# Pooled attention and two feed-forward layers: second batch's first steps held back by two units, value tails in three buffers, y staged in the weight sums' buffer, last sums stored by sync

## The chip, the core and the metric

One core of a Trainium2 chip runs the whole program. The metric is the device time of one execution in microseconds (us); less is better. The core's engines are TensorE (PE in the profile, with its weight loads as PEld), VectorE (DVE), ScalarE (ACT), GpSimd (POOL) and SyncE (SP), which issues nearly all DMAs. Each engine works through its own instructions in the order in which the program writes them and waits for the others by semaphores.

## What is computed

```python
k_p = k.reshape(B, H, Sp, pool, D).mean(axis=3)      # B, H, S, D = 8, 8, 576, 64; pool = 8, Sp = 72
v_p = v.reshape(B, H, Sp, pool, D).mean(axis=3)
attn = softmax(scale * q @ k_p.T)
x = (attn @ v_p) as 4608 tokens x 512
h = x @ w_in                                         # 512 x 2048
y = (h * clip(h + 3, 0, 6) / 6) @ w_out              # 2048 x 512
g = y @ w_gate; val = y @ w_val                      # 512 x 1536 each
out = (silu(g) * val) @ w_out2                       # 1536 x 512
```

The weights arrive as float64 words and are turned into fp32 on the chip. All products are taken in fp32 precision, as three products of a high and a low part (`mm3`, `split`).

## The kernel before

The work stands in one hand-written order (`manual_schedule`): a line that comes later in the program is queued later on its engine.

**Attention and first layer, up half.** Tokens go in nine blocks `j` of 512 (`NB`). Block 0's attention runs alone at the start. From then on, while TensorE makes the 16 products `up(hp, wu[f], x_tile(j))` of block `j` (one for each group `f` of 128 columns of `w_in`), `attn_slot` runs the attention of block `j + 1` in between, two slots for each `f`. The attention is cut into 84 units (a head pair and some rows), and each unit into steps with one letter: P brings q into the transposed layout (`prep_q`), RK and K pool and transpose k, R0 and R1 pool v and v's tail on GpSimd, R and Q split v, S are the scores, X A N M the softmax, E F T U L V W Y the transposes and the product with v. `when` and `when_startup` give each step a due time of unit number plus lag, and `steps` is sorted by it. So the list decides what stands ahead of what on every engine, and `block_end[j]`, the place of a block's last Y, decides which steps are done before block `j`'s products begin. Unit 8 and 9 are the last 64 rows of batch 0; unit 10 is the first of batch 1.

**Loads of the attention.** A load is put off by a number of steps after the step that frees its buffer (`later`): q of segment `i + 2` 12 steps after P of segment `i`, v's tail two heads and v three heads ahead, both 4 steps after Q. The tails have two buffers (`vts_t`), v has three. All are issued by SP in that order. R1 (tail of head h) and R0 (v of head h + 1) stand one behind the other on GpSimd, ahead of F of a unit with an even number (VectorE has the odd ones); F makes the low part of the unit's tail columns, which T's second transposes on TensorE (line 563) need.

**Weights.** In block 0 `weights.convert` brings one more group of `w_in` per `f`: ScalarE rescales a fetched tile, VectorE joins the words, and SP fetches the next into the freed tile. The other weights are turned into seven sums per tile by `prep_step` in steps spread over the blocks (`prep_slot`); tiles `q7` and `s7` hold a tile and its sums, and the sums go to memory. The gated block is stored by `store_g` from four `g32` tiles, one `f` behind.

**First layer, down half (stage b).** It runs for all nine blocks after the last up products, in seven products a block (`down_b`, n = 0 to 6). Its first operands, ten loads of 1 MB (`first_loads`: four `gq` tiles, six halves of `pw` tiles), are issued in `f` = 0 to 9 of the last block, and eight more halves directly after it. `split_b` makes the high and low parts, `evac_b` adds the products up to y and stores y; in the last block y is stored from ScalarE's queue. Four weight pieces are still prepared in this stage.

**Second layer.** It runs in six groups `p` of 768 tokens. `load_y` brings y into a tile, `x_step` makes seven operands in `xc` (quarters 11, 12, 21, 22 and their differences T1 to T4) by a copy on ScalarE (line 147), a subtraction on VectorE (line 148) and a difference (line 210). `up2` (line 694) takes them in the order 11, T2, T1, 21, T4, T3, 22. Weights for it come through four `wr` ring tiles (`load_next`). All these tiles are laid out where stage b's `gq`, `pw`, `stg`, `q7` and `s7` tiles stood, so their first loads wait until those have been read. At the change from stage b to the second layer the first group's `load_y`, `load_next` and `x_step`s are placed by hand behind n = 5 and n = 6 of the last block, after `evac_b`.

Of the kernel before, what the change touches and what calls it, by code (L numbers as in the profile page):

```python
# [23 lines left out]
def kernel(  # L24
# [27 lines left out]
    nc = tc.nc  # L52
# [25 lines left out]
    prep_ctx = ExitStack()  # L78
    stg_p = prep_ctx.enter_context(tc.tile_pool(name="stg", bufs=3, side="right"))
    q7_p = prep_ctx.enter_context(tc.tile_pool(name="q7", bufs=1, side="right"))  # L80
    s7_p = prep_ctx.enter_context(tc.tile_pool(name="s7", bufs=1, side="right"))
# [133 lines left out]
    WH = WC // 2  # L215
    prep_t = {}
# [12 lines left out]
    def prep_step(u, step):  # L229
# [21 lines left out]
        elif step in (2, 3):  # L251
            if step == 2:
                prep_t["f", u] = q7_p.tile([P, 8, WH], F32, tag="q7", name="q7")
# [8 lines left out]
        elif step in (5, 6):  # L262
            if step == 5:
                prep_t["s", u] = s7_p.tile([P, 7, 2, WH], F32R, tag="s7", name="s7")
# [31 lines left out]
    vts_t = [a_p.tile([96, POOL, D], F32, name=f"vts{i}") for i in range(2)]  # L296
    vmask = a_p.tile([P, 2, D], F32, name="vmask")
# [24 lines left out]
    def load_vtail(b, p, eng):  # L322
        v1 = v[b, 2 * p + 1].rearrange("(s o) d -> s o d", o=POOL)
        vts = vts_t[p % 2]
# [111 lines left out]
    def prep_v(b, p):  # L436
# [4 lines left out]
            out=m, in0=t[:, 0:1].to_broadcast([P, 2, D]), in1=vmask, op=ALU.mult  # L441
# [202 lines left out]
    def load_y(p):  # L644

        t = l2["ys"].tile([P, 4, 2, M], F32, tag="ys", name="ystg")
# [6 lines left out]
    def x_step(p, n, lo_eng, sum_eng):  # L653
# [4 lines left out]
        what, then = [("11", "T1"), ("22", "T3"), ("T1", "T2"), ("21", "T4"), ("T2", None), ("T3", None), ("T4", None)][n]  # L658
        x = xc[p, what] = l2["x"].tile([P, 2, 2, M], F32R, tag="x" + what, name="xc")
# [164 lines left out]
    lb = {}  # L824
# [54 lines left out]
    def evac_b(j, n):  # L879
# [91 lines left out]
    events = []  # L971
    for i in range(NU):
        startup_unit = i < unit_end[0]
        lag = dict(when_startup if startup_unit else when)
# [8 lines left out]
        events += [(i + lag[st[0]][0], lag[st[0]][1], st[1], n, st) for n, st in enumerate(stages)]  # L983
# [20 lines left out]
    for i, h in ((i, head_no[u[0], p]) for i, u in enumerate(units) for p in u[1]):  # L1004
# [8 lines left out]
        if h + 2 < len(heads) and h >= KT - 1:  # L1013
            before(("Q", h), ("R1", h + 2))
# [297 lines left out]
```

## Time and profile before

| | us |
|---|---|
| median of 3 runs | 1797.77 (1796.95 to 1799.96) |
| profiled execution | 1801.43 |
| its span | 1799.6 |
| PE busy in it | 1717.7 (95%) |
| DVE, ACT, POOL busy | 1336.2, 754.4, 634.7 |
| mean granted TensorE clock | 0.979 of full speed |

Matmuls of lines 609, 873 and 694 (up half, stage b, second layer) make nearly all of PE's time. TensorE is the engine that is nearly always busy; the time that can be won lies in its waits and in stretches where its granted clock is low.

### The profile page before, as it was taken

What the parts mean: (1) busy time and instruction counts of PE and PEld (TensorE: products, weight loads), DVE (VectorE), ACT (ScalarE), POOL (GpSimd) and SP (SyncE); (2) the same over time, 40 slices, a digit from 0 to 9 for tenths busy, and PEclk for the clock granted to TensorE, in tenths of its full rate; (3) what the DMA queues carried; (4) which work ended last, traced back from release to release, by engine and by line L of the source; (5) the groups of instructions that cost most, each with busy time, mean ns of one, the idle gap of its engine ahead of it and who ended that gap; (6) DMA issues with size and microseconds to landing.
All of it is one profiled execution on the core that took longest, in us unless ns stands there. A gap on an engine that the chain in (4) does not pass through costs nothing.

```text
span 1799.6 us, 30919 instructions
## 1 busy us (share of the span) xinstructions
PE 1717.7 (95%) x11209; PEld 1618.0 (90%) x11209; DVE 1336.2 (74%) x2356; ACT 754.4 (42%) x1657; POOL 634.7 (35%) x812
## 2 busy tenths in 40 slices
PE   4789998999999899999999899999999999999999
PEld 3568877877878699999999799999999999999999
DVE  6587887888886378888887578668568668668666
ACT  6464554555554345555554224225124124224222
POOL 6246665666732000000000252352351361450550
PEclk8799999999999999999999899999999999999999
DMA  7576878787777985554454787977977977878876
GB/s 167 123 188 174 250 227 261 237 258 229 221 225 274 393 328 187 183 182 147 161 203 150 263 275 246 318 269 244 320 256 249 328 251 257 316 247 274 274 246 214
DMA packets 235833, 432.47 MB, mean 240 GB/s; under 512 B 86689, under 2 KB 168609, under 8 KB 218529
## 3 DMA queue, kind: packets, MB, share of 16 engines
q1 hardware_dynamic: 233536, 429.20, 72.3%
q8 instruction: 88, 1.44, 0.3%
q10 hardware_dynamic: 2144, 1.31, 0.2%
q14 instruction: 65, 0.52, 0.1%
HBM read 326.11 MB, written 104.33 MB: 239 GB/s over the span
## 4 chain that ended last, share of the span: by engine, by line
PE 69%; DMA 8%; DVE 4%; issue 1%; SPq 1%; ACT 1%; POOL 1%; ACTq 0%; DVEq 0%; POOLq 0%
PE b L694 44%; PE b L873 17%; PE h L609 7%; DMA pw<-sw 1%; DMA wstg<-in_moe_w_out_dram 1%; DMA g<-g 1%; DVE g L625 1%; DMA gq<-g 1%; DMA wstg<-in_moe_w_val_dram 1%; DVE s L269 1%; DMA y<-o 1%; DMA q_in<-in_q_dram 0%; PE pss L489 0%; SPq L374 0%; DMA vts<-in_v_dram 0%
## 5 line engine op out<-in xcount | busy, mean ns | idle before, releaser
L694 PE MATMUL b<-xc,wr 128*128 128x384 f32 x3024 | 528.5, 335 | 8.6 <-ACT xc L147 5.4
L694 PEld LDWEIGHTS b<-xc,wr 128*128 128x128 f32 x3024 | 526.4, 189 | 9.5 <-ACT xc L147 5.8
L609 PE MATMUL h<-x,wu 128*128 128x512 f32 x1728 | 436.7, 404 | 9.2 <-DVE g L625 8.8
L741 POOL TENSOR_TENSOR s<-s,c 128x384 f32<-128x384 f32 x144 | 142.5, 1014 | 773.6 <-ACT s L739 773.6
L703 DVE TENSOR_TENSOR c<-c,b 128x384 f32<-128x384 f32 x504 | 265.2, 552 | 178.7 <-PE b L694 153.2
L609 PEld LDWEIGHTS h<-x,wu 128*128 128x128 f32 x1728 | 323.3, 193 | 78.5 <-DVE g L625 13.2
L873 PE MATMUL b<-gb,pw 128*128 128x256 f32 x3024 | 364.2, 283 | 3.4 <-ACT gb L147 2.8
L873 PEld LDWEIGHTS b<-gb,pw 128*128 128x128 f32 x3024 | 363.6, 192 | 4.1 <-ACT gb L147 3.0
L694 PE MATMUL b<-wr,gc 128*128 128x256 f32 x2268 | 265.6, 279 | 0.0
L694 PEld LDWEIGHTS b<-wr,gc 128*128 128x128 f32 x2268 | 265.4, 188 | 0.0
L147 ACT CAST gb<-gq 128x512 fp32r<-128x512 f32 x252 | 155.6, 621 | 170.2 <-PE b L873 159.1
L148 DVE TENSOR_TENSOR gb<-gq,gb 128x512 fp32r<-128x512 f32 x252 | 168.3, 688 | 64.0 <-ACT gb L147 63.3
L748 POOL TENSOR_TENSOR gf<-s,c 128x384 f32<-128x384 f32 x144 | 168.3, 1194 | 67.4 <-DVE c L703 64.8
L147 ACT CAST gc<-gf 128x768 fp32r<-128x768 f32 x126 | 105.7, 839 | 187.2 <-POOL gf L748 101.3
L739 ACT ACTIVATE s<-c 128x384 f32<-128x384 f32 x144 | 73.6, 526 | 204.6 <-DVE c L703 203.3
L148 DVE TENSOR_TENSOR gc<-gf,gc 128x768 fp32r<-128x768 f32 x126 | 134.1, 1096 | 15.6 <-ACT gc L147 13.9
L620 ACT ACTIVATE t<-h,half 128x512 f32<-128x512 f32 x144 | 99.2, 689 | 85.3 <-PE h L609 50.8
L625 DVE SCALAR_TENSOR_TENSOR g<-t,h 128x512 f32<-128x512 f32 x144 | 97.5, 677 | 33.5 <-DMA g<-g 23.5
L711 ACT COPY c<-b 128x384 f32<-128x384 f32 x72 | 33.9, 471 | 143.9 <-PE b L694 143.9
L851 DVE TENSOR_TENSOR gq<-gq 128x1024 f32<-128x1024 f32 x72 | 87.7, 1219 | 0.0
L537 POOL TENSOR_TENSOR e<-e,sm 128x288 f32<-128x288 f32 (+4 forms) x73 | 47.4, 649 | 110.1 <-DVE sm L533 85.5
L489 PE MATMUL pss<-kbd,qT 128*128 128x144 f32 (+2 forms) x320 | 58.1, 304 | 20.2 <-DVE qT L471 16.5
(106 smaller groups left out, 1673.1 us busy)
## 6 DMA issues: line engine op xcount, KB each, us to landing
wr<-sup SPq DMA_DIRECT2D x72, 1024.0 KB
wr<-sdn SPq DMA_DIRECT2D x84, 768.0 KB
wr<-sup SPq DMA_DIRECT2D x72, 768.0 KB
g<-g SPq DMA_DIRECT2D x144, 256.0 KB
gq<-g SPq DMA_DIRECT2D x36, 1024.0 KB
sup<-s SPq DMA_DIRECT2D x12, 1792.0 KB
wstg<-in_moe_w_out_dram SPq DMA_DIRECT2D x56, 256.0 KB
sw<-s SPq DMA_DIRECT2D x8, 1792.0 KB
```

Of the source, the lines that this page charges most:

```text
L147: nc.scalar.copy(out=hi, in_=src)
L148: lo_engine.tensor_tensor(out=lo, in0=src, in1=f32(hi), op=ALU.subtract)
L609: nc.tensor.matmul(out=ps, lhsT=w(kt, wh), rhs=x(kt, xh), start=first and n == 0, stop=last and n == 3 * len(kts) - 1,)
L620: nc.scalar.activation(out=t, in_=ps, func=ACTF.Relu, bias=half, scale=1.0 / 6.0)
L625: nc.vector.scalar_tensor_tensor(out=g, in0=t, scalar=1.0, in1=ps, op0=ALU.min, op1=ALU.mult)
L694: nc.tensor.matmul(out=ps, lhsT=w(wh), rhs=x(xh), start=first and n == 0, stop=last and n == 2)
L703: add = lambda dst, a, b: nc.vector.tensor_tensor(out=dst, in0=a, in1=b, op=ALU.add)
L739: nc.scalar.activation(out=g[q], in_=c[q], func=ACTF.Sigmoid)
L741: nc.gpsimd.tensor_tensor(out=g[q], in0=g[q], in1=c[q], op=ALU.mult)
L748: nc.gpsimd.tensor_tensor(out=gf[p][:, GP[TURN[q]], f], in0=g[q], in1=c[q], op=ALU.mult)
L851: nc.vector.tensor_tensor(out=v(what), in0=v(a), in1=v(b), op=op)
L873: nc.tensor.matmul(out=ps[:, d], lhsT=w[:, CB * c + k, wh, P * d:P * (d + 1)], rhs=g[:, gh, k], start=what == place and (c, d, k, m) == (0 ...
```

## The change

- **Steps.** From the first unit of batch 1 on, every step's due time is two units later (`held`). The list of steps of blocks 2 to 8 stays as it is. Six steps leave the startup for block 0: K4, RK5 (which does nothing, since TensorE pools k of heads 5 to 7), P8, S10, X10 and A10; RK4, with the load of k that follows it, moves back within the startup; the first steps of block 0 follow in another order.
- **Loads.** q is loaded 8 steps after P and not 12. v's tails have three buffers and are loaded three heads ahead. `vmask` is one column, read as a broadcast.
- **Last block's loads.** The ten `first_loads` go at `f` = 0, 1, 3, 4, 6, 8, 9, 11, 12, 14.
- **Change of stages.** `q7` and `s7` stay for good; y is staged in `s7`, the operand 11 in `q7`, the other operands in pools `xa`, `xb`, `xt`. `load_y(0)` is written behind n = 3, the two first `load_next` ahead of n = 5's and n = 6's evacuation, and `x_step`s 0 and 1 to 3 too; steps 4, 5 and 6 follow the loop. The order of the operands is 11, 22, T1, T2, 21, T4, T3, in all groups. y of the last block is stored by SP, its last three stores after x_step 5. The early activation that loaded the Sigmoid table is gone.

```diff
-    vts_t = [a_p.tile([96, POOL, D], F32, name=f"vts{i}") for i in range(2)]
-    vmask = a_p.tile([P, 2, D], F32, name="vmask")
+    vts_t = [a_p.tile([96, POOL, D], F32, name=f"vts{i}") for i in range(3)]
+    vmask = a_p.tile([P, 2, 1], F32, name="vmask")
...
-        vts = vts_t[p % 2]
+        vts = vts_t[(b * KT + p) % 3]
...
-        t = l2["ys"].tile([P, 4, 2, M], F32, tag="ys", name="ystg")
+        t = f32(new_s7("ystg"))[:, :8 * M].rearrange("p (q k n) -> p q k n", q=4, k=2)
...
-        what, then = [("11", "T1"), ("22", "T3"), ("T1", "T2"), ("21", "T4"), ("T2", None), ("T3", None), ("T4", None)][n]
-        x = xc[p, what] = l2["x"].tile([P, 2, 2, M], F32R, tag="x" + what, name="xc")
+        what, then = [("11", "T1"), ("22", "T3"), ("T1", "T2"), ("T2", None), ("21", "T4"), ("T4", None), ("T3", None)][n]
...
-            (nc.scalar if last else nc.sync).dma_start(out=y_d[:, 2 * c:2 * c + 2, t0:t0 + MB], in_=ob[tag])
+            send = lambda t=ob[tag]: nc.sync.dma_start(out=y_d[:, 2 * c:2 * c + 2, t0:t0 + MB], in_=t)
+            if last and n >= 5:
+                last_y.append(send)
+            else:
+                send()
...
+    batch1 = next(i for i, u in enumerate(units) if u[0])
+        held = i + 2 if i >= batch1 else i
-        events += [(i + lag[st[0]][0], lag[st[0]][1], st[1], n, st) for n, st in enumerate(stages)]
+        events += [(held + lag[st[0]][0], lag[st[0]][1], st[1], n, st) for n, st in enumerate(stages)]
...
-        for load, ahead in ((load_vtail, 2), (load_v, 3)):
-            for h in next_heads(i, ahead):
+        for load in (load_vtail, load_v):
+            for h in next_heads(i, 3):
...
-                    later.append((done[0] + 12, lambda n=n: load_q(segs[n], sync4)))
+                    later.append((done[0] + 8, lambda n=n: load_q(segs[n], sync4)))
...
-        first_loads = dict(enumerate([
+        first_loads = dict(zip((0, 1, 3, 4, 6, 8, 9, 11, 12, 14), [
...
+            if j == NB - 1 and n >= 5:
+                if n == 5:
+                    right_b.close()
+                    prep_ctx.close()
...
+                load_next()
+                for step in ((0,), (1, 2, 3))[n - 5]:
+                    x_step(0, step, nc.vector, nc.vector)
             evac_b(j, n)
             prep_slot(F1 * (NB - 1) + i)
-            if j == NB - 1 and n >= 5:
-                if n == 5:
-                    nc.scalar.activation(out=warm, in_=half, func=ACTF.Sigmoid)
...
-                    load_y(0)
-                    load_next()
-                for step in ((0, 1, 2), (3, 4, 5, 6))[n - 5]:
-                    x_step(0, step, nc.vector, nc.vector)
-        load_next()
+            if (j, n) == (NB - 1, 3):
+                assert not prep_at
+                load_y(0)
+        for step in (4, 5):
+            x_step(0, step, nc.vector, nc.vector)
+        for send in last_y:
+            send()
         left_b.close()
+        l2["xt"] = ctx.enter_context(tc.tile_pool(name="xt", bufs=1, side="right", reuse_waits="tile"))
+        x_step(0, 6, nc.vector, nc.vector)
```

## Rows read from the trace of the kernel before

**Rows 1.** The page, part 1: busy us, share of the span, instructions.

```profile
PE 1717.7 (95%) x11209; PEld 1618.0 (90%) x11209; DVE 1336.2 (74%) x2356; ACT 754.4 (42%) x1657; POOL 634.7 (35%) x812
```

**Rows 2.** Waits of PE, whole span: for whom; us in total, times, longest.

```profile
PE pss L489 <- DVE qT L471: 16.5, 5, 8.1
PE pst L563 <- POOL et L552: 13.4, 6, 5.3
PE h L609 <- DVE g L625: 8.8, 7, 4.3
PE b L694 <- ACT xc L147: 5.4, 1, 5.4
```

**Rows 3.** Timeline of DVE, startup: start, us, instruction [idle before, and its releaser].

```profile
50.97 0.24 DVE L471 STREAM_TRANSPOSE qT<-q_in 128x64 f32<-128x64 f32 x1 [9.04 <-DMA q_in<-in_q_dram]
52.81 0.24 DVE L471 STREAM_TRANSPOSE qT<-q_in 128x64 f32<-128x64 f32 x1 [1.60 <-DMA q_in<-in_q_dram]
...
60.09 0.65 DVE L471 STREAM_TRANSPOSE qT<-q_in 128x448 f32<-128x448 f32 x1 [3.99 <-DMA q_in<-in_q_dram]
```

**Rows 4.** Timeline of SP's DMA issues, startup.

```profile
39.48 2.68 SPq L326 DMA_DIRECT2D vts<-in_v_dram  x6
...
47.71 3.65 SPq L374 DMA_DIRECT2D q_in<-in_q_dram  x8
...
54.65 4.43 SPq L374 DMA_DIRECT2D q_in<-in_q_dram  x8
```

**Rows 5.** Timeline of PE: the first product of the up half.

```profile
64.26 4.93 PE L609 MATMUL h<-x,wu 128*128 128x512 f32 x12
```

**Rows 6.** Window of block 0: us, busy of each engine (instructions), PE clock, DMA share, GB/s.

```profile
64.00:140.00 76.00, 68.00 (x410) 56.28 (x409) 60.23 (x129) 46.05 (x164) 37.80 (x59) 0.95 0.64 171
```

**Rows 7.** Timeline of POOL: v's tails and v, at two of PE's waits.

```profile
297.33 2.52 POOL L433 TENSOR_TENSOR vts<-vts 96x256 f32<-96x256 f32 x3 [4.52 <-DVE mx L499]
299.82 2.31 POOL L433 TENSOR_TENSOR v_in<-v_in 128x256 f32<-128x256 f32 x3
...
432.25 1.66 POOL L433 TENSOR_TENSOR vts<-vts 96x256 f32<-96x256 f32 x3 [6.23 <-DVE aT L579]
```

**Rows 8.** Timeline of SP's DMA issues at the first of them.

```profile
293.14 1.60 SPq L326 DMA_DIRECT2D vts<-in_v_dram  x3
294.94 0.30 SPq L319 DMA_DIRECT2D v_in<-in_v_dram  x1
```

**Rows 9.** Timeline of SP's DMA issues at the beginning of stage b.

```profile
630.51 4.64 SPq L839 DMA_DIRECT2D pw<-sw  x8
636.53 8.05 SPq L121 DMA_DIRECT2D wstg<-in_moe_w_out_dram  x4
```

**Rows 10.** Windows: end of the up half, and stage b's beginning.

```profile
615.00:620.00 5.00, 3.62 (x9) 2.85 (x10) 3.05 (x4) 1.19 (x2) 0.00 (x0) 0.50 1.02 400
...
625.00:630.00 5.00, 5.00 (x36) 4.60 (x35) 2.70 (x5) 2.65 (x5) 0.00 (x0) 1.00 0.70 258
...
655.00:660.00 5.00, 1.89 (x12) 1.49 (x11) 1.27 (x3) 3.11 (x6) 0.00 (x0) 0.91 0.75 299
```

**Rows 11.** Timelines at the change from stage b to the second layer.

```profile
986.48 1.90 SPq L650 DMA_DIRECT2D ystg<-y  x4
990.40 1.40 DVE L889 TENSOR_TENSOR o<-o,b 128x512 f32<-128x512 f32 x2
992.33 1.28 ACT L1238 ACT_TABLE_LOAD   x1 [2.08 <-DVE o L889]
996.49 1.30 PE L694 MATMUL b<-xc,wr 128*128 128x384 f32 x6 [1.69 <-DMA wr<-sup]
1001.61 2.30 ACT L147 CAST xc<-ystg 128x768 fp32r<-128x768 f32 x3 [4.21 <-DMA y<-o]
1004.34 2.69 DVE L148 TENSOR_TENSOR xc<-ystg,xc 128x768 fp32r<-128x768 f32 x3
1005.35 16.92 PE L694 MATMUL b<-xc,wr 128*128 128x384 f32 x82 [1.43 <-DVE xc L148]
```

**Rows 12.** Window: the second layer's first matmuls.

```profile
1005.00:1010.00 5.00, 4.65 (x15) 4.65 (x16) 3.14 (x5) 0.67 (x2) 0.00 (x0) 0.50 0.01 3
```

More of the change, by code (lines that the diff above doesn't have):

```diff
@@ L78 @@
     prep_ctx = ExitStack()
+    s7_p = ctx.enter_context(tc.tile_pool(name="s7", bufs=1, side="right"))
+    q7_p = ctx.enter_context(tc.tile_pool(name="q7", bufs=1, side="right"))
     stg_p = prep_ctx.enter_context(tc.tile_pool(name="stg", bufs=3, side="right"))
-    q7_p = prep_ctx.enter_context(tc.tile_pool(name="q7", bufs=1, side="right"))
-    s7_p = prep_ctx.enter_context(tc.tile_pool(name="s7", bufs=1, side="right"))
     ident = const.tile([P, P], F32, name="ident")
@@ L215, with new_q7, new_s7 @@
     WH = WC // 2
+    def new_q7(name):
+        return q7_p.tile([P, 8 * WH], F32R, tag="q7", name=name)
+    def new_s7(name):
+        return s7_p.tile([P, 14 * WH], F32R, tag="s7", name=name)
     prep_t = {}
@@ L252, in prep_step @@
             if step == 2:
-                prep_t["f", u] = q7_p.tile([P, 8, WH], F32, tag="q7", name="q7")
+                prep_t["f", u] = f32(new_q7("q7")).rearrange("p (s n) -> p s n", s=8)
             s, at = prep_t["q", u].pop(0)
@@ L263, in prep_step @@
             if step == 5:
-                prep_t["s", u] = s7_p.tile([P, 7, 2, WH], F32R, tag="s7", name="s7")
+                prep_t["s", u] = new_s7("s7").rearrange("p (s a n) -> p s a n", s=7, a=2)
             q, t, part = prep_t["f", u], prep_t["s", u], slice(0, 4) if step == 5 else slice(4, 7)
@@ L657, in x_step @@
         v = lambda what: t[:, place[what]]
-        what, then = [("11", "T1"), ("22", "T3"), ("T1", "T2"), ("21", "T4"), ("T2", None), ("T3", None), ("T4", None)][n]
-        x = xc[p, what] = l2["x"].tile([P, 2, 2, M], F32R, tag="x" + what, name="xc")
+        what, then = [("11", "T1"), ("22", "T3"), ("T1", "T2"), ("T2", None), ("21", "T4"), ("T4", None), ("T3", None)][n]
+        if what == "11":
+            x = new_q7("xc")[:, :4 * M].rearrange("p (a k n) -> p a k n", a=2, k=2)
+        else:
+            pool = l2["xa" if what in ("T1", "22") else "xt" if what == "T3" else "xb"]
+            x = pool.tile([P, 2, 2, M], F32R, tag="x" + what, name="xc")
+        xc[p, what] = x
         split(x[:, 0], x[:, 1], v(what), lo_eng)
@@ L823 @@
     NCB = NP1 // CB
-    lb = {}
+    lb, last_y = {}, []
     gq, gb, bb, ob = {}, {}, {}, {}
@@ L1012 @@
             before(("K", h), ("RK", h + 2))
-        if h + 2 < len(heads) and h >= KT - 1:
-            before(("Q", h), ("R1", h + 2))
+        if h + 3 < len(heads) and h >= KT - 1:
+            before(("Q", h), ("R1", h + 3))
     for i, u in enumerate(units):
@@ L1187 @@
                     attn_ctx.close()
-                    for nm in ("gq", "px"):
+                    for nm in ("px", "gq"):
                         lb[nm] = right_b.enter_context(
@@ L1233 @@
                 load_g(j + 1, slot)
+            if j == NB - 1 and n >= 5:
+                if n == 5:
+                    right_b.close()
+                    prep_ctx.close()
+                    for nm, bufs in (("xa", 1), ("ring", 4), ("xb", 1)):
+                        l2[nm] = ctx.enter_context(
+                            tc.tile_pool(name=nm, bufs=bufs, side="right", reuse_waits="tile"))
+                load_next()
+                for step in ((0,), (1, 2, 3))[n - 5]:
+                    x_step(0, step, nc.vector, nc.vector)
             evac_b(j, n)
             prep_slot(F1 * (NB - 1) + i)
-            if j == NB - 1 and n >= 5:
-                if n == 5:
-                    nc.scalar.activation(out=warm, in_=half, func=ACTF.Sigmoid)
-                    right_b.close()
-                    prep_ctx.close()
-                    assert not prep_at
-                    for nm, to, bufs in (("xc", "x", 1), ("ys", "ys", 1), ("wr", "ring", 4)):
-                        l2[to] = ctx.enter_context(
-                            tc.tile_pool(name=nm, bufs=bufs, side="right", reuse_waits="tile"))
-                    load_y(0)
-                    load_next()
-                for step in ((0, 1, 2), (3, 4, 5, 6))[n - 5]:
-                    x_step(0, step, nc.vector, nc.vector)
-        load_next()
+            if (j, n) == (NB - 1, 3):
[5 more added lines that the diff above has]
+            send()
         left_b.close()
+        l2["xt"] = ctx.enter_context(tc.tile_pool(name="xt", bufs=1, side="right", reuse_waits="tile"))
+        x_step(0, 6, nc.vector, nc.vector)
         for nm, bufs in (("gf", 1), ("gc", 6), ("t", 1), ("o", 1)):
```

7 lines of the change are left out of this document (4 added, 3 removed).

## The prediction

> **What bounds the kernel.** I read the engines' busy time first: TensorE works 95% of the span [rows 1], so at most some 80 us can be won, and only where TensorE waits or its clock is low. The list of TensorE's waits says where: for the transposed q, 16.5 us in five waits; for `et`, the low part of the tails that GpSimd or VectorE makes, 13.4 in six; for the gated block `g` in the up half, 8.8 in seven; for the first operands of the second layer, 5.4 in one [rows 2]. The reader should see that each of these is a place in the program and not a rate. I then read the timelines at those places, the windows there for the granted clock, and SP's issues, since most of these waits end with a DMA. The change touches all four, so I sum by place: A startup, B value tails, C the end of the up half, D the change of stages. The up and down products themselves stay the same, and from block 2 on the order of the steps does too.
>
> **A, startup.** VectorE stands still 9.04 and 1.60 us for the q of segments 6 and 7 and 3.99 for that of segment 8 [rows 3]. The first two come late because SP issues them at 47.71 to 51.36, behind six tail loads that begin at 39.48 and six v loads [rows 4]. Loading q 8 steps after P puts them ahead of the tails in the written list. If they take the tails' place at 39.48, their issue ends at 43.1 (39.48 + 3.65); from the end of their issue to the last transpose it was 52.81 - 51.36 = 1.45, so that transpose goes to 44.6: 8.2 earlier. P8 then leaves the startup with its wait and its own time, 3.99 + 0.65 = 4.6. Together the first up product, now at 64.26 [rows 5], comes 12.8 earlier.
>
> What is given back: behind the waiting loads on SP are now nine tail loads and not six (0.45 each by 2.68 / 6, so 1.3 more), then v, and only then the next fetch of `w_in`; the two long q loads, 4.43 us of issue [rows 4], follow it as before. ScalarE's rescale waits for that fetch, and behind the rescale on ScalarE stand the copies of x that the first product needs at its end. Before, the fetch had slack, because VectorE stood still meanwhile. I bound this by zero and by 8.9 (two fetches in turn, each late by the whole 4.43), and take 3, nearer to the lower end: 1.3 for the tails, and a bit under half of one 4.43, since issuing and moving overlap. The moved steps themselves (one q transpose of 0.65, one reduction, four exponentials) lie in block 0, where VectorE is busy 60.23 of 76 us and TensorE 68.00 [rows 6]; free time there covers 1 to 2 us of VectorE's. If it didn't, A would lose them one for one. Holding the second batch back costs nothing further, since block 1's end and all later blocks keep their list. A gains 9.5 (4 to 14; the upper end lets nothing be given back and part of the other two q waits go).
>
> **B, value tails.** At 297.33 and 432.25 GpSimd has been idle 4.52 and 6.23 us when it pools a tail [rows 7]. The profile names an instruction of VectorE that ended just then, but the pooling of a tail reads nothing except what its DMA brings, and at the first place that DMA was issued at 293.14 [rows 8]; so I take the DMA. With three buffers and three heads of lead this tail is there one head earlier, and that wait goes. But what is late next stands right behind it: v of the next head is issued at 294.94, 1.8 us after the tail and still only then, and GpSimd pools it at 299.82, directly behind the tail [rows 7, 8]. If v lands as long after its issue as the tail does (4.2 at the first place), it is there at 299.1, and F behind it moves by 0.7; if it lands with the tail, by 2.5. I take 1 us at each of the two large waits, and 1 for the others and for the clock after them: 3. The lower bound is zero (v's DMA ends the wait alone); the upper is 12, nearly all of `et`'s 13.4. Loading q four steps earlier can bring the tail and v forward on SP, which speaks for more than zero. The third buffer costs one more memset at the start, before the first data lands, and the narrower mask the same multiplications.
>
> **C, end of the up half.** `g` waits because its store is late and its four buffers are then full: the ten loads of 1 MB in ten successive `f` stand ahead of the stores. The largest wait is 4.3 of the 8.8 [rows 2]; behind it the window 615 to 620 shows a granted clock of 0.50, the lower level of 1.2 GHz, in 3.62 us of work [rows 10], so 1.8 more. DMA share there is 1.02 at 400 GB/s, 2.6 us for 1 MB. Spread over 15 `f`, seven loads and not ten are issued by `f` = 9, 7.8 us of queue less, which is more than the wait; so wait and clock loss go, 6, and 1 of the smaller ones. What is late next is the other end: three loads now fall in the last five `f`, so the queue is not empty when the eight bulk `pw` loads are issued at 630.51 and the `wstg` fetch behind them at 636.53 [rows 9]. A rescale on ScalarE waits for that fetch, with stage b's copies behind it: TensorE works only 1.89 of 5 us at 655 to 660 [rows 10]. Free DMA time at 625 to 630 is 0.30 of 5 us; it was cover, and it goes. I price the delay at 2 us (0 to 6: three loads at 2.6 less that cover). C gains 5 (1 to 8).
>
> **D, change of stages.** TensorE waits 1.69 for `wr`, 5.4 for a copy of ScalarE and 1.43 for the low part [rows 2, 11], 8.5 in all, and then runs at clock 0.50: 15 matmuls in 4.65 us [rows 12], 0.31 each, where 82 later take 16.92 (0.21 on average, the slow ones among them) [rows 11]. First, y: it is loaded at 986.48 because its tile lies on tiles still read; `s7` is free far earlier, so this load and, in the same way, the first `wr` tiles move ahead of stage b's end, and the 1.69 goes. Second, ScalarE: its copies stood 4.21 behind the store of y that it issues itself [rows 11], with the operand T2, the second needed, fifth in the list. Third, the Sigmoid table: its load of 1.28 stood before the first copies [rows 11]; it comes back at the first Sigmoid, where ScalarE is not the bound and GpSimd alone waits.
>
> What is late next is VectorE. Between the two additions `o`, which it begins at 990.40, and T2's low part the new list has, besides those additions (0.7 each by 1.40 / 2), the low parts of 11, 22, T1, T2 and the differences T1, T3, T2: seven at 0.9 (2.69 / 3) [rows 11], 6.3, and in the chain one copy of 0.77: 990.4 + 1.4 + 6.3 + 0.8 = 998.9. P1 can begin at 994.8 (996.49 - 1.69) and takes 1.3, so TensorE waits 2.8 (996.1 to 998.9). Before it was free for good at 1005.35, with one matmul of P6 done: 6.4 later. T4's low part follows 4.2 behind T2's (addition, low part of 21, difference, copy, low part); P6, P5 and P2 are 18 matmuls, 3.1 us at the fast pace and 5.6 at 0.31, so it costs between 0 and 1.1. I expect the clock to fall again after a wait of 2.8 as it did before, so I count no gain there. D gains 6 (3 to 8: the wait for T4 and two more of VectorE's operations, or a clock that stays up). SP's last three stores wait for VectorE's last addition; behind them on SP is only the third `load_next`, whose tile isn't free earlier, so this costs nothing; if it did, it would be what a ring tile is late by.
>
> The Trainium skill, page "DMA: Bandwidth & Descriptors", section "Issuing engines are not separate DMA queues", says that DMAs from any engine run on the same 16 DMA engines and that issuing from another saves only issue time. By that rule alone moving the stores to SP would win TensorE nothing, D would be about 2 and the time 1778. The row differs: 4.21 us of ScalarE stood behind its own issue, so here issue time is what counts.
>
> **Sum.** 9.5 + 3 + 5 + 6 = 23.5. The profiled execution took 1801.43 (span 1799.6), so it would become 1777.9; the median of 1797.77 stands 3.7 lower, and from there it is 1774.3. I predict 1774. All lower ends together give a gain of 8 (1790), all upper ends 42 (1756).
>
> **Rivals.**
> - The startup's gain is given back in block 0, because the `w_in` fetch or VectorE is the bound there; or q of segments 6 and 7 still lands late and only P8's 4.6 is won. A is then 4: 1780. For it: VectorE's 79% in rows 6. Against: most of what moves is waiting, not work. 15%.
> - The tails were the whole wait, v being in time: B is 12 and the time 1765. For it: idle times of 4.52 and 6.23. Against: v's issue behind the tail. 13%.
> - The last block's transfers are late anyway and the wait only moves into stage b: C is 0 and the time 1779. For it: share 1.02 [rows 10]. 9%.
> - Slower: the q loads now stand four steps earlier on SP, so SP may wait there for the P that frees the buffer, with the stores of `g` behind it, and TensorE for `g`. Nine blocks lie between 64 [rows 5] and about 627 (stage b has begun in the window 625 to 630 [rows 10]), 62.5 us each, with some 150 steps; four steps are 1.7 us. From 0.43 us for each of the 55 q loads after the startup it eats the whole gain; at half of 1.7 it costs 47: 1821. Against: a wait for q's buffer is nowhere among the large ones now. 5%.
> - None of the places pays more than its lower bound and a new wait of 8 or so takes that too: 1798. 3%.
>
> The forecast itself (1766 to 1782) has 55%.
>
> **Range and chances.** The range takes in the first three rivals and most of the bounds: 1760 to 1789. A measurement of this kernel can tell about 0.2%, 3.6 us. Faster 0.91, same 0.04, slower 0.05.
>
> **What would show it.** A: the first product of line 609 at 51 to 55, no idle time of VectorE over 3 us before it. B: POOL's idle time before `vts` gone, a short one before `v_in` in its place, and `et`'s waits at 10 us. C: no wait over 1 us for `g` after 570, and a longer hole some 30 us into stage b. D: a hole of 3 us after six matmuls of line 694, none for `wr`. Wrong would be: `et`'s waits nearly gone (B), or a first product at 60 or later (A), or new waits for `wu`.

## The result and the profile after

The changed kernel takes **1768.83 us** (median of 4 runs, 1768.66 to 1772.04) beside 1797.55 for the kernel before (4 runs, 1796.95 to 1799.96): ratio **0.984 (0.9825 to 0.9859)**, 28.7 us less. The forecast was 1774, a gain of 23.8.

The profiled execution of after took 1768.66 (span 1766.9, granted clock 0.987), 0.2 below its median; that of before stood 3.9 above its median. So the two traces lie 32.7 apart and the medians 28.7: some 4 us of what the traces show below are no gain of the change, and no run tells in which place they lie. Line numbers of the profile move with the change: the up half's product is L616 (L609 before), `et`'s transpose L570 (L563), stage b L885 (L873), the second layer L706 (L694).

The waits of TensorE in the trace of after (for whom; us in total, times, longest), to be read beside [rows 2]:

```profile
PE pst L570 <- POOL et L559: 8.4, 6, 2.3
...
PE b L885 <- ACT gb L147: 7.4, 1, 7.4
...
PE pss L496 <- DVE qT L478: 2.8, 4, 1.6
...
PE h L616 <- DVE g L632: 2.5, 3, 1.2
PE b L706 <- ACT xc L147: 2.3, 1, 2.3
...
PE psv L594 <- ACT aTt L580: 1.9, 1, 1.9
PE h L616 <- ACT x L605: 1.7, 1, 1.7
```

All four of the named waits are smaller: q 16.5 to 2.8, `et` 13.4 to 8.4, `g` 8.8 to 2.5, the second layer's operands 5.4 to 2.3. Three are new or clearly larger: `gb` in stage b (2.8 before, in one wait), and two for copies of ScalarE at the start, `aTt` just ahead of the first up product and x in the middle of it.

Where the 32.7 us lie, from the times at which the same matmul, by its count, starts in both traces (each us from the span's start):

| matmul | before | after | after earlier by | of this place |
|---|---|---|---|---|
| first up product | 64.3 | 50.1 | 14.2 | A won 14.2 |
| block 1 begins | 144.7 | 136.7 | 8.0 | A gave back 6.2: **8.0** |
| block 8 begins | 573.5 | 552.0 | 21.6 | B: **13.6** |
| stage b begins | 627.1 | 595.7 | 31.4 | C won 9.9 |
| 337th matmul of stage b | 672.3 | 646.5 | 25.8 | C gave back 5.7: **4.2** |
| 43rd matmul of the second layer | 1014.0 | 981.2 | 32.7 | D: **7.0** |

From there to the end nothing more changes. The forecast had A 9.5, B 3, C 5, D 6.

Startup in the trace of after, timelines of VectorE, SP, ScalarE and TensorE (beside [rows 3 to 5]):

```profile
42.07 0.24 DVE L478 STREAM_TRANSPOSE qT<-q_in 128x64 f32<-128x64 f32 x1 [2.01 <-DMA q_in<-in_q_dram]
...
37.93 3.74 SPq L381 DMA_DIRECT2D q_in<-in_q_dram  x8
41.71 4.12 SPq L333 DMA_DIRECT2D vts<-in_v_dram  x9
...
48.43 0.39 SPq L121 DMA_DIRECT2D wstg<-in_moe_w_in_dram  x1
...
54.33 0.65 ACT L133 ACTIVATE wstg<-wstg 128x512 f32<-128x512 f32 x1 [4.92 <-DMA wstg<-in_moe_w_in_dram]
...
50.06 3.54 PE L616 MATMUL h<-x,wu 128*128 128x512 f32 x9
55.29 1.22 PE L616 MATMUL h<-x,wu 128*128 128x512 f32 x3 [1.69 <-ACT x L605]
...
63.17 4.59 PE L616 MATMUL h<-x,wu 128*128 128x512 f32 x12
68.86 3.01 PE L616 MATMUL h<-x,wu 128*128 128x512 f32 x12
```

The q loads stand ahead of the tails and VectorE's 9.04 is 2.01. But the fetch of `w_in` stands behind nine tails and six v loads, at 48.43; ScalarE waits 4.92 for it and TensorE, in the middle of its first product, 1.69 for the copy behind. Then the second product, at 63.17, takes 4.59 where the third takes 3.01.

Stage b in the trace of after, in windows (columns as in [rows 6]; beside [rows 10]):

```profile
620.00:625.00 5.00, 5.00 (x44) 5.00 (x43) 0.69 (x1) 1.11 (x2) 0.00 (x0) 1.00 1.02 423
625.00:630.00 5.00, 0.67 (x6) 0.47 (x4) 0.00 (x0) 0.00 (x0) 0.00 (x0) 0.97 1.03 395
630.00:635.00 5.00, 1.75 (x6) 1.46 (x7) 1.92 (x3) 3.37 (x6) 0.00 (x0) 0.50 0.56 229
```

The timeline of TensorE in after, there and at the change of stages (beside [rows 11, 12]):

```profile
633.10 12.14 PE L885 MATMUL b<-gb,pw 128*128 128x256 f32 x84 [7.43 <-ACT gb L147]
...
968.93 1.22 PE L706 MATMUL b<-xc,wr 128*128 128x384 f32 x6
972.48 0.45 PE L706 MATMUL b<-xc,wr 128*128 128x384 f32 x1 [2.33 <-ACT xc L147]
973.48 26.81 PE L706 MATMUL b<-xc,wr 128*128 128x384 f32 x144 [0.55 <-DVE xc L148]
```

The hole of 7.43, where before had one of 2.77, is nearly all that C gave back: up to the 337th matmul TensorE stands idle 8.5 us and not 3.1. The clock is 0.50 (1.2 GHz) behind it, but it was low behind the smaller hole too (0.75 from 660 to 665 of before). The second layer now begins without a wait for `wr` and stands 2.88 behind six matmuls (2.33, and 0.55 after one more).

### The profile page after: what moved, and what is told of

Same layout as the page of the kernel before. It is cut to its first block, busy times and chain, and to the rows that moved or that the text cites. A ratio compares the mean times of both kernels' runs of the same rounds, so it can differ in the third digit from the quotient of the medians.

```text
span 1766.9 us, 30932 instructions
## 1 busy us (share of the span) xinstructions
PE 1710.7 (97%) x11209; PEld 1615.9 (91%) x11209; DVE 1333.0 (75%) x2356; ACT 753.8 (43%) x1656; POOL 634.5 (36%) x813
## 4 chain that ended last, share of the span: by engine, by line
PE 81%; DMA 8%; DVE 6%; ACT 2%; SPq 1%; issue 1%; POOL 1%; DVEq 0%; ACTq 0%; POOLq 0%
PE b L706 45%; PE b L885 18%; PE h L616 14%; DMA g<-g 3%; PE pss L496 1%; DMA pw<-sw 1%; DMA gq<-g 1%; DVE g L632 1%; DMA wstg<-in_moe_w_out_dram 1%; SPq L381 1%; DMA qv<-in_q_dram 1%; PE pst L570 1%; PE pst L566 1%; DVE s L276 0%; DVE mx L506 0%
## 5 line engine op out<-in xcount | busy, mean ns | idle before, releaser
L706 PE MATMUL b<-xc,wr 128*128 128x384 f32 x3024 | 527.3, 335 | 2.9 <-ACT xc L147 2.3
L706 PEld LDWEIGHTS b<-xc,wr 128*128 128x128 f32 x3024 | 525.5, 188 | 3.5 <-ACT xc L147 2.7
L616 PE MATMUL h<-x,wu 128*128 128x512 f32 x1728 | 430.6, 400 | 4.2 <-DVE g L632 2.5
L616 PEld LDWEIGHTS h<-x,wu 128*128 128x128 f32 x1728 | 320.3, 191 | 70.2 <-DVE g L632 3.7
L885 PE MATMUL b<-gb,pw 128*128 128x256 f32 x3024 | 364.6, 283 | 8.8 <-ACT gb L147 7.4
L885 PEld LDWEIGHTS b<-gb,pw 128*128 128x128 f32 x3024 | 363.7, 192 | 9.8 <-ACT gb L147 7.6
L706 PE MATMUL b<-wr,gc 128*128 128x256 f32 x2268 | 265.6, 279 | 0.0
L706 PEld LDWEIGHTS b<-wr,gc 128*128 128x128 f32 x2268 | 265.4, 188 | 0.0
L148 DVE TENSOR_TENSOR gc<-gf,gc 128x768 fp32r<-128x768 f32 x126 | 134.3, 1095 | 16.5 <-ACT gc L147 14.3
L205 DVE TENSOR_TENSOR gf<-gf 128x768 f32<-128x768 f32 (+1 forms) x66 | 67.0, 1030 | 12.2 <-POOL gf L760 10.9
```

Source lines behind the costliest of these rows:

```text
L148: lo_engine.tensor_tensor(out=lo, in0=src, in1=f32(hi), op=ALU.subtract)
L616: nc.tensor.matmul(out=ps, lhsT=w(kt, wh), rhs=x(kt, xh), start=first and n == 0, stop=last and n == 3 * len(kts) - 1,)
L706: nc.tensor.matmul(out=ps, lhsT=w(wh), rhs=x(xh), start=first and n == 0, stop=last and n == 2)
L885: nc.tensor.matmul(out=ps[:, d], lhsT=w[:, CB * c + k, wh, P * d:P * (d + 1)], rhs=g[:, gh, k], start=what == place and (c, d, k, m) == (0 ...
```

## Experiments

Times are medians. A ratio, its interval and a gain given behind it are against runs of the kernel before on the same chip (medians 1795.5 to 1797.5); shifts within a trace are against the trace of before, or of after where that is said. One caution comes from the runs themselves: the startup of `only_spread` below is that of before, unchanged, and yet reaches block 1 2.5 us earlier. A single shift of that size proves nothing.

### B: tails, or q?

**only_tails**: the kernel before with the three buffers, the three heads of lead and the narrow mask.

```diff
-    vts_t = [a_p.tile([96, POOL, D], F32, name=f"vts{i}") for i in range(2)]
+    vts_t = [a_p.tile([96, POOL, D], F32, name=f"vts{i}") for i in range(3)]
...
-        for load, ahead in ((load_vtail, 2), (load_v, 3)):
-            for h in next_heads(i, ahead):
+        for load in (load_vtail, load_v):
+            for h in next_heads(i, 3):
```

> The kernel before with three tail buffers, tails loaded three heads ahead and the one-column mask; nothing else of the change. Between the first product of block 1 and the first of block 7 the changed kernel gained 13.6 us, where I had predicted 3. Theory V (as predicted: v of the next head, issued behind the tail, is the next late thing): this kernel gains 2 to 4 us there, POOL's idle time moves from before the tails to before v. Theory T (the tails were nearly the whole wait): it gains 9 to 13 there, and the time is 1785 to 1789.

1793.46, ratio 0.9984 (0.9971 to 0.9997): 2.9 us (0.5 to 5.2). From block 2 to block 8 its trace gains 7.9, between theory V's 2 to 4 and theory T's 9 to 13, so both miss there; `et`'s waits sum to 9.7. By the time the tails alone are worth little. GpSimd's idle time does move from the tail to v behind it, as theory V had it (timeline of GpSimd, beside [rows 7]):

```profile
296.14 3.18 POOL L433 TENSOR_TENSOR v_in<-v_in 128x256 f32<-128x256 f32 x3 [3.48 <-DMA v_in<-in_v_dram]
```

**after_two_tails**: the buffers and the lead undone in the changed kernel (the mask stays narrow).

> The changed kernel with two tail buffers and tails two heads ahead again. Theory V: it loses 2 to 4 us against the changed kernel between blocks 1 and 7, since the rest of the 13.6 there comes from q loaded earlier. Theory T: it loses 9 to 13 there (time 1778 to 1782), with idle times of POOL of 4 us and more before tails at two places or more.

1772.71, ratio 0.9871 (0.9834 to 0.9909). From block 2 to 8 it gains 13.1, where after gains 13.6. With q loaded early the third buffer is worth 0.5 in the trace, less than either theory had; the time, from two runs, isn't told apart from after's.

**after_q12**: the changed kernel with q loaded 12 steps after P, as before.

```diff
-                    later.append((done[0] + 8, lambda n=n: load_q(segs[n], sync4)))
+                    later.append((done[0] + 12, lambda n=n: load_q(segs[n], sync4)))
```

> The changed kernel with q loaded 12 steps after P again. Startup, by the prediction: q of segments 6 and 7 stands behind tails and v once more, the first product of the up half comes about 8 us later than in the changed kernel, and VectorE has one idle time of 8 to 9 us there. Blocks 1 to 7: theory V wants a loss of 6 or more there as well, theory T less than 4.

1777.24, ratio 0.9897 (0.9858 to 0.9935). Between block 2 and 8 only 7.1 are left of 13.6, a loss of 6.4 as theory V wanted.

**only_q8**: the opposite, q 8 steps after P and nothing else.

> The kernel before with one edit: q of a segment after the startup is loaded 8 steps after its predecessor's P and not 12. Theory Q (SP issues in order; with 12 steps the four q loads of a segment, 2 to 3 us of issue, stand right ahead of the next tail and v, and that is what made GpSimd's v late): from the second to the eighth up product the gain is 11 to 13 us, as with the whole change, although the tails have two buffers; et's waits on TensorE fall from 13.4 to 7 to 9. At the start the first up product comes about 7 earlier, but segment 8 is still in the startup, so no more than 2 of it is left at block 1. Time 1779 to 1786. Rival S (q and tails add up, as after_q12's 7 and after's 13.6 would have it): 6 us in that stretch, et's waits at 10, time 1787 to 1791. Rival N (q matters only at the start): 1793 or more.

1788.46, ratio 0.9947 (0.9927 to 0.9967): 9.5 us (5.9 to 13.1). Between block 2 and 8 its trace gains 12.0, as theory Q had it, with two buffers for the tails, and `et`'s waits are 7.7. The trace speaks for Q and against S (6 us there, waits of 10). The median doesn't: it is 2.5 above Q's range and inside S's; the profiled run, 1784.8, is the fastest of the four, inside Q's. At the start it missed: the first up product comes 2.2 earlier and not 7, since VectorE, with q of segments 6 and 7 early, then waits 8.75 for that of segment 8.

What the earlier q does is seen at the largest wait for `et`. In the kernel before, timeline of TensorE (v is issued at 294.94, [rows 8]):

```profile
303.25 0.66 PE L563 MATMUL pst<-ident,et 128*96 128x128 f32 x2 [5.28 <-POOL et L552]
```

In only_q8, timelines of SP and TensorE:

```profile
284.41 0.38 SPq L319 DMA_DIRECT2D v_in<-in_v_dram  x1
...
290.88 0.42 PE L563 MATMUL pst<-ident,et 128*96 128x128 f32 x2 [0.61 <-POOL et L552]
```

In after, timelines of SP, GpSimd and TensorE:

```profile
281.15 0.38 SPq L326 DMA_DIRECT2D v_in<-in_v_dram  x1
...
284.52 2.53 POOL L440 TENSOR_TENSOR v_in<-v_in 128x256 f32<-128x256 f32 x3 [3.70 <-DVE e L516]
...
288.57 0.66 PE L570 MATMUL pst<-ident,et 128*96 128x128 f32 x2 [2.28 <-POOL et L559]
```

Start less wait is the moment at which TensorE asks for `et`: 297.97 before, and v was issued 3.0 ahead of it. The same two rows in all six kernels:

| kernel | q after P | tail buffers | v issued ahead of TensorE's request | wait |
|---|---|---|---|---|
| before | 12 | 2 | 3.0 | 5.28 |
| only_tails | 12 | 3 | 3.2 | 4.44 |
| after_q12 | 12 | 3 | 3.0 | 4.41 |
| only_q8 | 8 | 2 | 5.9 | 0.61 |
| after_two_tails | 8 | 2 | 5.6 | 1.27 |
| after | 8 | 3 | 5.1 | 2.28 |

The lag of q splits the six, the tail buffers don't. SP issues almost without a pause here: from 244 to 294 of before its issues take 39 of the 50 us, and the gaps between them are mostly 0.04 to 0.2 us. With q's loads earlier, v is issued some 2.5 us earlier for TensorE. The likely path is that SP does the q loads while it is not yet late; that v's issue follows the lag is shown, this path is argued.

### A: holding back, and what block 0 takes

**after_not_held**: the changed kernel with the second batch's steps where they were.

```diff
-        held = i + 2 if i >= batch1 else i
+        held = i
```

> The changed kernel without the two units of delay for the second batch (held = i). By the prediction's step, P8 and its wait come back into the startup: first product 3 to 5 us later than in the changed kernel; blocks from 2 on unchanged. What reaches the end of block 0: theory H (the six moved steps cost block 0 about what they saved) wants the end of block 0 within 1.5 us of the changed kernel; theory C (block 0 gives back because the w_in fetch is late and TensorE's clock stays low) wants 2 to 5 us later.

1774.35, ratio 0.988 (0.9852 to 0.9909). Its startup waits 9.9 us for q of segment 8; its first product comes 12.3 later than after's, where 3 to 5 were expected, and block 1 begins 2.0 earlier than before, against 8.0 in after: 6.0 of loss, outside both theories' ranges. So holding is worth 6 of A. Loading q early is worth next to nothing at block 1: after_q12, in which TensorE still waits 8.2 for q of segments 6 and 7, begins block 1 7.4 earlier than before, although its first product is 7.3 later than after's. Block 0 takes the difference back. At the first product the two edits need each other: early q alone brings it 2.2 earlier (only_q8), the change without early q 6.9 (after_q12), both together 14.2.

**after_v_behind**: the changed kernel, the first tails and v of the second batch 14 steps later, so that the fetch of `w_in` passes them.

```diff
-                later.append((done[0] + 4, lambda load=load, h=h: load(*heads[h], nc.sync)))
+                later.append((done[0] + (18 if i == KT - 1 else 4), lambda load=load, h=h: load(*heads[h], nc.sync)))
```

> The changed kernel, with the first tail and v loads of the second batch (SP at 41.71 to 48.3) asked for 14 steps later, so that the fetch of w_in at 48.43 goes ahead of them. Theory K (what block 0 gives back is the lower clock: the fetch behind those loads makes ScalarE wait 4.92, TensorE 1.69, and the granted clock, which had risen to 1.00 at 53, falls to 0.50 from 57 to 66): ScalarE's wait falls below 2, TensorE's goes, the second up product begins at 57 to 59 and not at 63.17, block 1 begins 4 to 7 earlier, time 1762 to 1765. Rival W (the wait alone, and the clock falls at the next short wait anyway): 1 to 2 us, time 1767 to 1768. Rival L (the tails and v are late where they now stand, or the next fetch is): 0 or a loss, 1769 to 1772.

1768.55, ratio 0.9841 (0.9822 to 0.9859): theory K missed; the time lies between rival W's range and L's, 0.3 from after's. The fetch is issued at 44.61, the wait of 1.69 is gone; q of segment 8, now behind the tails and v at 52.13, makes TensorE wait 2.81. The second product starts at 62.77.

**after_tails_last**: only the tails go behind, and behind q of segments 8 and 9 as well.

```diff
+                behind = i == KT - 1 and load is load_vtail
-                later.append((done[0] + 4, lambda load=load, h=h: load(*heads[h], nc.sync)))
+                later.append((done[0] + (34 if behind else 4), lambda load=load, h=h: load(*heads[h], nc.sync)))
```

> The changed kernel; of the second batch's first loads only the nine tail loads move, behind the next w_in fetches and the q of segments 8 and 9 (v stays). The tails are first read at about 71, so nothing should wait for them. after_v_behind left the question open: its 1.69 wait went, a wait of 2.81 for the q of segment 8 came, and the lower clock from 59 to 65 stayed. Here both loads are early. Theory K (a pause of 1.7 to 2.8 us, whatever its cause, costs the clock of the next ten us): no wait over 1 us on TensorE between 50 and 65, clock 1.00 from 53 on, second up product at 57 to 59 and not at 63.17, block 1 begins 4 to 6 earlier, time 1763 to 1765. Rival W (the clock falls here anyway, or another wait of this size takes the place): 0 to 2 us, 1767 to 1769.

1766.35, ratio 0.9824 (0.98 to 0.9847), not told apart from after's; theory K missed again. No wait of TensorE between 50 and 65 is over 0.53 any more, and still the clock falls. Three windows of 6 us each show it (the clock is the third number from the end). In after:

```profile
50.00:56.00 6.00, 4.31 (x13) 3.00 (x12) 2.84 (x3) 0.91 (x2) 2.83 (x5) 0.76 1.15 197
56.00:62.00 6.00, 5.60 (x39) 4.55 (x39) 2.48 (x6) 2.75 (x15) 0.00 (x0) 0.53 0.80 225
62.00:68.00 6.00, 6.00 (x28) 4.96 (x26) 0.90 (x2) 2.25 (x5) 0.00 (x0) 0.62 0.77 179
```

In after_tails_last:

```profile
50.00:56.00 6.00, 6.00 (x22) 4.60 (x21) 2.96 (x4) 1.24 (x4) 3.08 (x5) 0.55 0.83 186
56.00:62.00 6.00, 5.14 (x44) 4.38 (x43) 2.48 (x6) 3.36 (x17) 0.00 (x0) 0.73 0.52 102
62.00:68.00 6.00, 6.00 (x27) 5.03 (x26) 1.64 (x4) 1.56 (x4) 0.00 (x0) 0.70 0.92 215
```

In after_fetch_tails, the last experiment below, whose startup is written exactly as that of after_tails_last:

```profile
50.00:56.00 6.00, 6.00 (x21) 4.68 (x22) 3.80 (x7) 1.61 (x4) 3.49 (x6) 0.60 1.06 184
56.00:62.00 6.00, 5.13 (x52) 4.32 (x50) 2.48 (x6) 4.16 (x20) 0.00 (x0) 1.00 0.53 83
62.00:68.00 6.00, 6.00 (x39) 5.31 (x38) 4.52 (x10) 3.23 (x13) 1.94 (x3) 1.00 1.02 243
```

TensorE is busy for as long in after_tails_last as in after_fetch_tails, 17.1 of 18 us, and does 93 matmuls in the one and 112 in the other. From the first to the third up product it is 18.8 us in after (50.06 to 68.86), 16.9 in after_tails_last (50.31 to 67.20), 13.1 in after_fetch_tails (51.17 to 64.26) and 12.8 in after_q12 (57.33 to 70.14), whose clock is up from 60 on. From the first product to block 1 it is 80.4 in before, 86.6 in after, 84.7 in after_tails_last and 80.2 in after_fetch_tails. So of after's 6.2 some 2 are waits behind the late fetch, and some 4 the lower level of the clock; the moved steps cost about nothing, as far as single traces tell.

### C: the loads at the end of the up half

**only_spread**: the kernel before with its ten loads spread.

```diff
-        first_loads = dict(enumerate([
+        first_loads = dict(zip((0, 1, 3, 4, 6, 8, 9, 11, 12, 14), [
```

> The kernel before with one edit: the ten loads for the next stage are spread over 15 f. Theory C (the prediction's: wait for g goes, some comes back at the fetch behind the bulk loads): the end of the up half 9 to 10 us earlier, the hole at the copy of ScalarE in stage b grows from 2.8 to 7 or 8, 4 us net, time about 1791. Rival M (transfers are late either way): net within 1, time about 1795. Nothing before the last block of the up half moves.

1794.62, ratio 0.9977 (0.9966 to 0.9989): 4.1 us (2.0 to 6.1). The median stands at rival M's 1795; the ratio and the parts in the trace are theory C's. The last block of the up half is 9.7 shorter, the hole in stage b grows from 2.77 to 7.84, and 3.7 are left: after's figures.

**after_fetch_first**: the changed kernel, the last two of the four pairs of bulk `pw` loads issued behind the fetch.

```diff
-        for n in (3, 4, 5, 6):
+        for n in (3, 4):
             for h in range(2):
                 load_pw(n, h)
...
             prep_slot(F1 * (NB - 1) + i)
+            if i == 0:
+                for n2 in (5, 6):
+                    for h in range(2):
+                        load_pw(n2, h)
```

> The changed kernel, with the last two of the four pairs of bulk pw loads at the start of stage b issued behind the fetch that a rescale on ScalarE waits for, and not ahead of it. Theory F (the hole of 7.43 us at 633 is that fetch behind 8 MB of bulk loads): the hole falls to 0 to 3 and the low clock behind it (0.50 in 630 to 635) goes: 5 to 9 us, 1760 to 1764. Rival P (the pw loads that now stand behind are late in their turn): a wait for pw in stage b, same time or slower. Rival R (the rescale waits for something else): hole stays, 1768 to 1769.

**1759.63**, ratio 0.9788 (0.977 to 0.9806), 9.2 below after: theory F, at the upper end of its 5 to 9. Its SP and ScalarE timelines and a window:

```profile
602.58 4.43 SPq L851 DMA_DIRECT2D pw<-sw  x4
608.59 2.35 SPq L121 DMA_DIRECT2D wstg<-in_moe_w_out_dram  x4
613.39 7.76 SPq L851 DMA_DIRECT2D pw<-sw  x4
...
622.26 0.67 ACT L133 ACTIVATE wstg<-wstg 128x512 f32<-128x512 f32 x1
...
625.00:630.00 5.00, 5.00 (x44) 5.00 (x44) 4.97 (x9) 2.24 (x5) 0.00 (x0) 1.00 1.02 421
```

In after the same rescale waits (timelines of SP and ScalarE):

```profile
601.34 8.29 SPq L851 DMA_DIRECT2D pw<-sw  x8
611.77 7.77 SPq L121 DMA_DIRECT2D wstg<-in_moe_w_out_dram  x4
...
630.57 0.65 ACT L133 ACTIVATE wstg<-wstg 128x512 f32<-128x512 f32 x1 [9.45 <-DMA wstg<-in_moe_w_out_dram]
```

The hole is gone, at the same DMA share (1.02 and 1.03), and no `pw` is late: only the order of the queue was wrong.

### D: who stores y

**after_store_act**: the changed kernel, y of the last block stored by ScalarE.

```diff
-            if last and n >= 5:
-                last_y.append(send)
+            if last:
+                nc.scalar.dma_start(out=y_d[:, 2 * c:2 * c + 2, t0:t0 + MB], in_=ob[tag])
             else:
                 send()
```

> The changed kernel, with the y stores of the last block issued by ScalarE again and not by SP; the order of the split steps stays as changed. Theory H (a store issued by ScalarE holds ScalarE until the addition it waits for is done, 4.21 us before): the copies of the second layer's operands come later, the wait of 2.3 us grows to 4 to 6, with the lower clock behind it 2 to 5 us more: 1771 to 1774. Rival O (the split steps now stand ahead of the last stores on ScalarE, so only the copies for the fourth product and later can be held): 0 to 1 us, 1768.5 to 1770. By the Trainium skill, page DMA: Bandwidth & Descriptors, section Issuing engines are not separate DMA queues, only the issue time differs, which would be O's value too.

1772.33, ratio 0.9863 (0.9842 to 0.9884), 3.5 above after: theory H in the time, though the wait is 3.73 and not 4 to 6. Timelines of ScalarE and TensorE:

```profile
968.34 1.09 ACTq L908 DMA_DIRECT2D y<-o  x2
969.47 1.57 ACT L147 CAST xc<-ystg 128x768 fp32r<-128x768 f32 x2 [3.26 <-DVE o L901]
...
974.82 0.44 PE L706 MATMUL b<-xc,wr 128*128 128x384 f32 x1 [3.73 <-ACT xc L147]
```

ScalarE has done no work for 3.26 when it comes to the copies. The two issues in that stretch take 0.37 each; the rest is waiting, nearly all for the additions that its own stores wait for. From stage b's end to the 43rd matmul of the second layer this costs 2.4 us, of 7.0.

### Together

**after_both**: after_fetch_first and after_v_behind in one.

> after_fetch_first and after_v_behind together. The two edits lie at the start and at stage b, with seven blocks between them, so their gains add: 9.2 (1768.8 less 1759.6) and whatever after_v_behind gives by itself: 1753 to 1756 by theory K, 1758 to 1759 by rival W, 1759.6 or more by rival L.

1757.88, ratio 0.9786 (0.9769 to 0.9804): not told apart from after_fetch_first, as rival W had it. But in its trace the clock stays at 1.00 from 55 to 70, through a pause of 1.33 us that ends at 58.56, and block 1 begins 3.0 earlier than in after.

**after_fetch_tails**: after_fetch_first and after_tails_last in one.

> The changed kernel with the two edits that paid: the last two pairs of bulk pw loads behind the fetch at the start of stage b (9.6 us in the trace of after_fetch_first), and the first tails behind the next w_in fetches and the q of segments 8 and 9 (1.9 in the trace of after_tails_last). If they add, 1757 to 1758; if the small one is noise between runs, 1759 to 1760. And on the open question of block 0's clock: theory S (the lower clock from 59 to 65 belongs to the order of steps there) has it again; theory R (it is chance from run to run) has it gone in some.

**1751.86**, ratio **0.975 (0.9735 to 0.9762)**, the fastest of all, 17.0 below the changed kernel, and more than the two parts add up to (11.7); the 1757 to 1760 of both expectations missed. Its trace has block 0's clock at 1.00 from 56 on, as shown above, and begins block 1 5.3 earlier than after's; after_tails_last, with the same startup, 1.6. That speaks against theory S. But the profiled execution, 1756.48, is the slowest of its five, and three took 1751.5 to 1751.9: what those gained besides, the trace doesn't show.

## Why the prediction was right, and where it was not

The sign and the four places came out, and three of the four sizes lie within 1.5 of the forecast, one of them by luck and one in part; 1768.83 lies in the forecast's own range. Point by point:

- **A, 9.5 forecast, 8.0 measured.** (The prediction's own terms, 12.8 less 3, make 9.8.) The gross gain was worked out as 12.8 and is 14.2: the transposes of q moved as written (42.07, with 2.01 of idle time ahead of it), P8 left. The term that was mis-sized is what is given back: 3 forecast, 6.2 measured. The two misses have opposite signs, which is the lucky part. The mechanism named (fetch behind tails and v, ScalarE behind the fetch, the first product behind ScalarE) is there, 4.92 and 1.69. What the sum left out is the clock: it falls to 0.50 and some 4 us go with it. "A given back" was a rival at 15%; half of it happened.
- **B, 3 forecast with 12 as the upper bound, 13.6 measured.** The step that failed is the last one: that loading q four steps earlier can bring the tail and v forward on SP was said, and given no price of its own. The rest was read rightly. GpSimd's idle time did move to `v_in` (3.70 at 284.52, none before `vts`), so v was the next late thing, and the third buffer alone is worth 2.9. But q's earlier issue, counted only in the startup and as a risk, moved v itself. The bound of 12 was wrong too, since it counted waits alone: from 300 to 310 of before the granted clock is 0.66, in after no ten us between 190 and 530 are under 0.91. Of the 13.6, 8.5 are waiting (TensorE is busy 323.4 of 340 us before, 331.9 after), about 5 the clock. The waits for `et` in these windows fall from 11.7 to 5.5; those for x and `g` bring the rest of the 8.5. So the sign that was to show B wrong, `et`'s waits nearly gone, didn't come although B was wrong.

The rows for this, from windows of 10 us: the one behind the largest wait and the sum of all 34. In before, from 200 to 540:

```profile
300.00:310.00 10.00, 6.75 (x24) 5.52 (x25) 5.66 (x14) 2.52 (x7) 5.73 (x10) 0.66 0.75 236
...
sum 340.00, PE 323.36 PEld 268.55 DVE 281.72 ACT 180.18 POOL 210.25; mean PE 9.51 PEld 7.90 DVE 8.29 ACT 5.30 POOL 6.18
```

In after, from 190 to 530:

```profile
290.00:300.00 10.00, 10.00 (x47) 8.19 (x45) 6.71 (x17) 4.39 (x13) 2.77 (x7) 0.91 0.93 292
...
sum 340.00, PE 331.87 PEld 277.51 DVE 288.26 ACT 184.87 POOL 216.62; mean PE 9.76 PEld 8.16 DVE 8.48 ACT 5.44 POOL 6.37
```

- **C, 5 forecast, 4.2 measured**, by luck, since two errors cancel: 9.9 won where 7 was said, 5.7 given back where 2 was said. On the side of the gain the clock was mis-sized: 5.8 us of idle time go from the last block, and 4.1 of TensorE's busy time, for which 1.8 was said. On the other side 2 was chosen between 0 and 6 without a row that speaks for it. The hole is 7.43, and the upper end was the right one: DMA share is about 1 from 600 to 630, right up to the end of the fetch's wait, so no cover was left.
- **D, 6 forecast, 7.0 measured.** The first matmul comes 1.9 earlier (1.69 said), TensorE stands 2.88 (2.8 said) and then runs on; T4's wait did not come. The clock fell less than before: 0.71 from 975 to 980, where it was 0.50 [rows 12]. after_store_act shows that the stores on SP are a good third of it: without them 2.4 of 7.0 go. The prediction read the 4.21 as time that ScalarE's own issue takes; that reading was wrong. In before the issue takes 0.37, and ahead of it ScalarE waits for VectorE's addition (timelines of VectorE and ScalarE before, beside [rows 11]):

```profile
999.92 0.68 DVE L889 TENSOR_TENSOR o<-o,b 128x512 f32<-128x512 f32 x1
1001.20 0.37 ACTq L894 DMA_DIRECT2D y<-o  x1
```

The Trainium skill, page "DMA: Bandwidth & Descriptors", section "Issuing engines are not separate DMA queues", holds that another issuer saves only the time of initiating a DMA, usually small beside the DMA itself. The trace agrees that the issue is short (0.37). What costs is the wait for the addition, which the issuing engine takes on with it, and all that stands behind it there: in after_store_act ScalarE does nothing for 3.26 around two such issues, and the kernel takes 3.5 us longer.

- **Slower through q's buffer** (5%): the first link of this rival came true. Ahead of the q loads SP now waits 21.9 us in all for VectorE, which makes P's transposes; in before it is 3.8, in only_q8 22.7, in after_q12 1.7. The largest group of them, among the waits of SP in after:

```profile
SPq L381 <- DVE mx L506: 11.6, 7, 3.3
```

It doesn't reach TensorE, whose waits for `g` fall from 8.8 to 2.5; the net effect of the earlier q is a gain.

- The sum of the four places is 9.2 short in the traces (23.5 against 32.7); B alone is 10.6 short. The time is only 5.2 off, because the profiled execution of before was slower than its median and that of after wasn't.

What stays open: why block 0's clock falls in some traces and not in others (after_tails_last and after_fetch_tails have one startup, after_v_behind and after_both another), and so how much of after_fetch_tails' last 8 us is its edit. The timed runs say that it is faster than after_fetch_first (intervals 0.9735 to 0.9762 and 0.977 to 0.9806), one trace each can't say why. D's other 4.6 us (`wr` and y earlier, the operands' order, the Sigmoid table) were not taken apart.

## What to carry to other kernels

Where one engine issues nearly all DMAs and is busy doing it, price a moved load by all that stands behind it on that engine, not by its own reader alone: here four steps for q were worth more than a third buffer for the tile that seemed to be waited for. Price a wait with the clock that follows it, both when it goes and when it comes. And put a small load that a chain waits for ahead of the bulk loads: two pairs of `pw` behind the fetch gave 9.2 us, and no load came late for it.

## What the hardware showed that was not expected

- The granted clock of a stretch can't be read off from its pauses. Between 56 and 66 us it fell from 1.00 (2.4 GHz) to 0.50 (1.2 GHz) with no pause over 0.53 on TensorE (after_tails_last), and stayed at 1.00 with pauses of 0.54 and 1.33 (after_both). From the first to the third up product it is 16.9 us in the one and 13.9 in the other.
- A row of SP that merges several DMAs is not issue time. The four of the `wstg` fetch stand as 2.35 us behind four bulk loads and as 7.77 behind eight, yet each takes SP 0.33 to issue in both. The rest is SP waiting: ahead of these four it stands 8.5 us in all in after until bulk loads issued before are done, and 1.6 in after_fetch_first. So a queue of bulk loads delays the issue of what follows, not only its landing.
- Two early loads can replace each other: three tail buffers gain 7.9 in the trace by themselves and 0.5 once q is early.
